# A new written-out order for the first half of a delta-rule and gated feed-forward kernel

## The chip, the cores and the metric

The kernel runs on one core of a Trainium2 chip. The metric is the device time of one execution in microseconds. Five engines run side by side: TensorE (PE in the profile, its weight loads PEld), VectorE (DVE), ScalarE (ACT), GpSimd (POOL) and SyncE (SP), which only issues transfers. Each engine works through its own instructions in the order in which the program gave them; semaphores make one engine wait for another.

## The reference, cut to what matters

```python
# q, k, v: (4, 8, 768, 48); beta: (4, 8, 768)
k_n = k / (norm(k) + 1e-06)
for t in range(768):                       # one state per batch and head
    y[t] = q[t] @ state
    v_old = k_n[t] @ state
    state = state + beta[t] * outer(k_n[t], v[t] - v_old)
x = y.transpose(0, 2, 1, 3).reshape(3072, 384)
h = x @ w_in                               # 384 x 2048
out = (h * cos(h)) @ w_out                 # 2048 x 384
```

All inputs are float32; the weights come as pairs of 32-bit words which the kernel joins to one.

## The kernel before, in words

The sequence is cut into 24 units of 32 steps (index n below); two units make a pair (index p or m, 12 of them), and one pair's outputs are the 256 tokens of one pass of the feed-forward part.

For a unit the kernel loads k, q and v (`("k", n)`, ...; `load`, L398), turns k and q (`turn`, or by blocks from memory: `("blocks", n, a)`, L417), forms the two Gram matrices (`gram`, L675; `gram_keys`, `gram_queries`) and needs the inverse of a triangular matrix made of the first. For units 0 and 1 that inverse is formed by repeated doubling on TensorE (`("double", n, level, par)`, L759, with copies on ScalarE, L767, and turns and adds on VectorE, L772 to L779). From unit 2 on it is formed for a pair at a time by column elimination on GpSimd: the Gram matrix goes to memory (`gram_put`, L833) and back in another layout (`gram_get`, L846 and L854), `eye` (L865, L867) sets the start, `("inv", m, i)` (L879, L886) are the steps, and the result goes to memory (`put`, L891) and back (`get`, L902 for pair 1 and L910 for the others). Of pair 1, the step `("inv", 1, 0)` runs on VectorE and the other three on GpSimd. The recurrence of a unit is then `state` (L930), `right`, `solve` (L996, L1002; for pair 1 it is `solve_half` and `between`, both L960, with `half_out` on ScalarE, L972, and `between_out` on VectorE, L980, after them), `solve_out` (L1014), `update` (L1027), `update_out`, `within` (L1045, L1057), `within_out` (L1070), `features` (L1078) and `features_out` (L1086). `norms` (L574), `scale` and `weigh` prepare the factors.

The feed-forward part of pair 0 is plain: `("hidden", 0, f)` (L1099) and `("out", 0, i, k)`. For the other pairs the first product is done as 20 block products, `("layer", p, x)` (L1273), of sums of the inputs, `("x_sum", p, name)` (L1188), the second as seven, `("out", p, step, part)` (L1355), with sums of gates `("left", p, x, s)` (L1371). `turns` (L1136), `rest` (L1143), `cos` (L1152) and `gate` (L1155) form h cos(h).

The weights arrive in 28 loads `("weights", t)` (L518): 12 of 512 KB for `w_in`, 16 of 384 KB for `w_out`. Each takes one of eight tiles of tag g, is split on ScalarE (`split`, L528 and L532), shifted on VectorE (`shift`, L536) and joined on GpSimd (`("add", t)`, L540), which frees the tile. The same eight tiles serve squares, gates and `half_out`.

`("warm", i)` (L495) is one matmul on data that nobody reads, a filler for TensorE; once an output product has begun it issues nothing:

```python
    def keep_warm():
        if not out_begun:
            nc.tensor.matmul(p_out[:, 0], ...)
```

There are five of them ahead of everything and 17 among the tasks.

All of this is written as 2199 tasks. `Order.add` registers a task under its key with its dependencies and the tiles it makes and uses; the costs, due times and engines that are handed to it are not used when the order is run. `Order.LINE` is the order itself: it names every task once, by its number in the order of registration, and `Order.run` calls them in that sequence. An engine therefore gets its instructions in the order of the line. `Order.run` also gives out the tiles: of a tag's free places the one that has been free longest. So the line also sets whose release a task waits for. `Order.OTHER` is a set of keys. A transfer whose key is in it is issued by ScalarE's queue, otherwise by SP's (`queue`); for `inv`, `x_sum`, `in_sums`, `left` and `right` it chooses between GpSimd and VectorE (`either`).

Of the kernel before, what the change touches and what calls it, by code (L numbers as in the profile page):

```python
# [59 lines left out]
class Order:  # L60

    OTHER = {
        ('v', 0), ('v', 1), ('gram_put', 2), ('gram_put', 3), ('inv', 1, 0), ('put', 1),
        ('gram_put', 4), ('v', 5), ('gram_get', 2), ('put', 2), ('gram_put', 6), ('v', 8),
        ('v', 9), ('blocks', 9, 0), ('blocks', 9, 1), ('put', 4), ('get', 10), ('v', 11),
        ('blocks', 11, 0), ('blocks', 11, 1), ('gram_put', 11), ('gram_get', 5), ('v', 12),
        ('gram_put', 13), ('gram_get', 6), ('get', 13), ('v', 14), ('blocks', 14, 0), ('v', 15),
        ('blocks', 15, 0), ('blocks', 15, 1), ('v', 16), ('gram_put', 16), ('v', 17), ('k', 18),
        ('v', 18), ('get', 18), ('v', 20), ('gram_put', 21), ('gram_get', 11), ('store', 0, 1),
        ('right', 4, 4), ('left', 1, 1, 0), ('left', 1, 3, 0), ('left', 1, 3, 1),  # L70
        ('store', 1, 0), ('store', 1, 1), ('x_sum', 2, 'd'), ('x_sum', 2, 'n'),
        ('x_sum', 2, 'm'), ('x_sum', 2, 'e'), ('x_sum', 2, 'k'), ('x_sum', 2, 'g'),
        ('x_sum', 2, 'i'), ('x_sum', 2, 'l'), ('x_sum', 2, 'f'), ('x_sum', 2, 'b0'),
        ('left', 2, 4, 1), ('left', 2, 3, 1), ('x_sum', 3, 'd'), ('x_sum', 3, 'n'),
        ('x_sum', 3, 'm'), ('x_sum', 3, 'e'), ('x_sum', 3, 'k'), ('x_sum', 3, 'g'),
        ('x_sum', 3, 'i'), ('x_sum', 3, 'l'), ('x_sum', 3, 'h'), ('x_sum', 3, 'b0'),
        ('left', 3, 4, 1), ('left', 3, 3, 1), ('store', 3, 0), ('store', 3, 1),
        ('x_sum', 4, 'd'), ('x_sum', 4, 'm'), ('x_sum', 4, 'g'), ('x_sum', 4, 'i'),
        ('left', 4, 3, 0), ('left', 4, 3, 1), ('x_sum', 5, 'd'), ('x_sum', 5, 'e'),
        ('x_sum', 5, 'l'), ('x_sum', 5, 'h'), ('x_sum', 5, 'b0'), ('left', 5, 2, 0),  # L80
        ('left', 5, 4, 1), ('left', 5, 3, 0), ('left', 5, 3, 1), ('x_sum', 6, 'd'),
        ('x_sum', 6, 'g'), ('x_sum', 6, 'l'), ('x_sum', 6, 'f'), ('x_sum', 6, 'b0'),
        ('left', 6, 1, 0), ('left', 6, 4, 0), ('store', 6, 0), ('x_sum', 7, 'd'),
        ('x_sum', 7, 'm'), ('x_sum', 7, 'g'), ('x_sum', 7, 'i'), ('x_sum', 7, 'f'),
        ('x_sum', 7, 'h'), ('x_sum', 7, 'b0'), ('left', 7, 4, 0), ('left', 7, 4, 1),
        ('left', 7, 3, 1), ('store', 7, 0), ('x_sum', 8, 'd'), ('x_sum', 8, 'm'),
        ('x_sum', 8, 'e'), ('x_sum', 8, 'k'), ('x_sum', 8, 'g'), ('x_sum', 8, 'l'),
        ('left', 8, 3, 0), ('store', 8, 0), ('store', 8, 1), ('x_sum', 9, 'd'),
        ('x_sum', 9, 'm'), ('x_sum', 9, 'e'), ('x_sum', 9, 'k'), ('x_sum', 9, 'i'),
        ('x_sum', 9, 'l'), ('x_sum', 9, 'b0'), ('left', 9, 1, 0), ('left', 9, 2, 0),  # L90
        ('left', 9, 1, 1), ('left', 9, 3, 0), ('store', 9, 1), ('x_sum', 10, 'k'),
# [1857 lines left out]
```

## Time and profile before

| | us |
|---|---|
| median of the runs (3) | 640.1 |
| lowest and highest | 638.85, 642.2 |
| profiled execution | 642.77 |
| its span, first to last instruction | 641.0 |

The profile is of one execution. Busy times and shares are of its span. In the list of groups a row gives line, engine, operation, the tile written and those read, the number of instructions, the busy time and the mean of one in ns, and the idle time just before them with what ended it. In the rows by stage the columns are from and to, the length, then for PE, PEld, DVE, ACT and POOL the busy time and the number of instructions, the mean granted clock of TensorE, the busy share of the DMA engines and GB/s. In the order of time a row begins with start and length. The chain of waits is followed back from the last instruction to whatever released each step.

### The profile page before, as it was taken

What the parts mean: (1) busy time and instruction counts of PE and PEld (TensorE: products, weight loads), DVE (VectorE), ACT (ScalarE), POOL (GpSimd) and SP (SyncE); (2) the same over time, 40 slices, a digit from 0 to 9 for tenths busy, and PEclk for the clock granted to TensorE, in tenths of its full rate; (3) what the DMA queues carried; (4) which work ended last, traced back from release to release, by engine and by line L of the source; (5) the groups of instructions that cost most, each with busy time, mean ns of one, the idle gap of its engine ahead of it and who ended that gap; (6) DMA issues with size and microseconds to landing.
All of it is one profiled execution on the core that took longest, in us unless ns stands there. A gap on an engine that the chain in (4) does not pass through costs nothing.

```text
span 641.0 us, 24058 instructions
## 1 busy us (share of the span) xinstructions
PE 612.1 (95%) x10096; PEld 571.4 (89%) x10096; DVE 504.4 (79%) x1051; ACT 297.5 (46%) x533; POOL 435.1 (68%) x791
## 2 busy tenths in 40 slices
PE   6978788999999999999999999999999999999997
PEld 4857777788799998999999999999999999999997
DVE  5876736999999897788878788978878676757872
ACT  3546535645543543543743553643544443635440
POOL 4428877788888888786886786888884881212231
PEclk8897979999999999999999999999999999999999
DMA  9876656655354645446234445333225011000001
GB/s 187 218 169 174 136 130 134 148 87 83 72 87 74 103 74 96 69 67 111 42 52 87 75 79 91 54 45 70 45 35 101 18 31 23 20 3 15 13 20 30
DMA packets 215844, 50.75 MB, mean 79 GB/s; under 512 B 207384, under 2 KB 210744, under 8 KB 215736
## 3 DMA queue, kind: packets, MB, share of 16 engines
q1 hardware_dynamic: 161132, 32.34, 27.8%
q10 hardware_dynamic: 54300, 16.33, 12.1%
q8 instruction: 79, 1.29, 0.8%
q0 software_dynamic: 304, 0.54, 0.4%
q14 instruction: 29, 0.24, 0.1%
HBM read 38.95 MB, written 10.22 MB: 77 GB/s over the span
## 4 chain that ended last, share of the span: by engine, by line
PE 76%; DMA 8%; POOL 5%; DVE 5%; issue 2%; SPq 2%; ACT 1%; ACTq 1%; DVEq 0%; POOLq 0%
PE p_out L1355 30%; PE p_h L1273 28%; PE p_kq L930 3%; PE p_s L1027 3%; POOL part L879 2%; POOL z L886 2%; PE p_u L1002 2%; PE p_kq L1057 2%; PE p_g L675 2%; PE p_h L1099 2%; DMA qp<-in_q_dram 2%; PE p_h L1355 2%; DMA kp<-in_k_dram 2%; PE p_z L1078 1%; DMA w_sum<-z_dr 1%
## 5 line engine op out<-in xcount | busy, mean ns | idle before, releaser
L879 POOL TENSOR_TENSOR part<-z,gb 128x126 f32<-128x126 f32 (+23 forms) x321 | 141.6, 441 | 44.1 <-DMA gb<-g_dr 17.5
L886 POOL TENSOR_TENSOR z<-z,part 128x126 f32<-128x126 f32 (+23 forms) x321 | 142.8, 445 | 25.2
L1355 PE MATMUL p_out<-w_out,g_ffn 128*128 128x192 f32 x672 | 121.0, 329 | 0.0
L1355 PEld LDWEIGHTS p_out<-w_out,g_ffn 128*128 128x128 f32 x672 | 107.9, 190 | 1.0
L1152 ACT ACTIVATE turns<-turns,halfpi 128x512 f32<-128x512 f32 x96 | 68.0, 718 | 83.2 <-DVE turns L1143 71.6
L1273 PE MATMUL p_h<-x_sum,w_in 128*128 128x128 f32 x704 | 92.3, 278 | 0.0
L1355 PE MATMUL p_out<-w_sum,g_ffn 128*128 128x192 f32 x496 | 88.7, 328 | 0.0
L1273 PEld LDWEIGHTS p_h<-x_sum,w_in 128*128 128x128 f32 x704 | 85.6, 191 | 1.9
L1136 ACT ACTIVATE turns<-g_ffn,quarter_turn 128x512 int32<-128x512 f32 x77 | 55.0, 719 | 66.3 <-DVE g_ffn L1155 35.4
L1355 PEld LDWEIGHTS p_out<-w_sum,g_ffn 128*128 128x128 f32 x496 | 79.6, 190 | 0.6
L1290 DVE TENSOR_TENSOR g_ffn<-g_ffn,p_h 128x512 f32<-128x512 f32 x88 | 59.5, 679 | 14.7 <-PE p_h L1273 13.7
L1155 DVE TENSOR_TENSOR g_ffn<-turns,g_ffn 128x512 f32<-128x512 f32 x77 | 61.7, 810 | 11.7 <-ACT turns L1152 11.6
L1143 DVE SCALAR_TENSOR_TENSOR turns<-g_ffn,turns 128x512 f32<-128x512 f32 x77 | 57.1, 750 | 8.2 <-ACT turns L1136 8.1
L1273 PE MATMUL p_h<-x_sum,in_sum 128*128 128x128 f32 x440 | 58.9, 278 | 0.8 <-POOL x_sum L1188 0.8
L1273 PEld LDWEIGHTS p_h<-x_sum,in_sum 128*128 128x128 f32 x440 | 54.3, 191 | 2.2 <-POOL x_sum L1188 1.0
L1070 ACT COPY y<-p_kq 32x384 f32<-32x384 f32 x96 | 45.1, 470 | 19.0 <-PE p_kq L1057 8.1
L1407 DVE SCALAR_TENSOR_TENSOR o<-p_out,o 128x192 f32<-128x192 f32 x74 | 25.1, 351 | 29.7 <-PE p_out L1355 29.5
L1273 PE MATMUL p_h<-x_ffn,w_in 128*128 128x128 f32 x352 | 46.6, 277 | 1.0 <-ACT p_h L1285 1.0
L1273 PEld LDWEIGHTS p_h<-x_ffn,w_in 128*128 128x128 f32 x352 | 43.0, 192 | 1.6 <-ACT p_h L1285 1.3
L574 POOL TENSOR_TENSOR knrm<-ksum,halves 128x16 f32<-128x16 f32 (+1 forms) x14 | 37.1, 2647 | 10.1 <-DVE ksum L562 9.5
L1371 POOL TENSOR_TENSOR g_ffn<-g_ffn 128x512 f32<-128x512 f32 x15 | 19.1, 1271 | 30.5 <-DVE g_ffn L1155 26.6
L1285 ACT COPY p_h<-p_h 128x512 f32<-128x512 f32 x44 | 25.3, 575 | 28.5 <-PE p_h L1273 20.4
(168 smaller groups left out, 1051.7 us busy)
## 6 DMA issues: line engine op xcount, KB each, us to landing
g_ffn<-in_moe_w_in_dram SPq DMA_DIRECT2D x7, 512.0 KB, 7.8
g_ffn<-in_moe_w_out_dram SPq DMA_DIRECT2D x9, 384.0 KB
kp<-in_k_dram SPq DMA_DIRECT2D x136, 24.0 KB, 2.5
gb<-g_dr SPq DMA_DIRECT2D x12, 256.0 KB, 3.9
g_ffn<-in_moe_w_out_dram ACTq DMA_DIRECT2D x7, 384.0 KB
g_ffn<-in_moe_w_in_dram ACTq DMA_DIRECT2D x5, 512.0 KB, 5.9
vp<-in_v_dram ACTq DMA_DIRECT2D x52, 48.0 KB, 2.7
zt<-z_dr SPq DMA_DIRECT2D x68, 32.0 KB, 2.7
```

Source lines behind the costliest of these rows:

```text
L574: nc.gpsimd.tensor_tensor(out=scales[m][2][:, part], in0=sums[m, part.start][:, 0:n], in1=halves[:, 0:n], op=ALU.pow,)
L879: eng.tensor_tensor(out=part, in0=z[:, 0:rows, j, None].to_broadcast(shape), in1=a[:, j, None, j + 1 :].to_broadcast(shape), op=ALU.mult,)
L886: eng.tensor_tensor(out=behind, in0=behind, in1=part, op=ALU.subtract)
L1070: nc.scalar.copy(by_parity(y[quarter(b)]), p_kq[quarter(b ^ 1), :, b % 2])
L1136: nc.scalar.activation(turns[p, f], hidden_of(p, f), AF.Identity, bias=quarter_turn, scale=TURN)
L1143: nc.vector.scalar_tensor_tensor(out=r, in0=hidden_of(p, f), scalar=TURN, in1=t, op0=ALU.mult, op1=ALU.subtract,)
L1152: nc.scalar.activation(r, r, AF.Sin, bias=halfpi, scale=2.0 * math.pi)
L1155: nc.vector.tensor_tensor(out=place(p, f), in0=step_of(rests.pop((p, f)), f), in1=step_of(hidden_of(p, f), f), op=ALU.mult,)
L1273: nc.tensor.matmul(p_h[:, e], in_block(*w)[:, e], x_of(p, b), start=new and e == 0, stop=True, skip_group_check=True,)
L1285: nc.scalar.copy(to, part_of(p, one))
L1290: nc.vector.tensor_tensor(out=part_of(p, to), in0=part_of(p, one), in1=part_of(p, two), op=op)
L1355: nc.tensor.matmul(p_o, left(p, part, a)[:, e % 4], right(e, b), start=(e == 0), stop=(e == FT // 2 - 1), skip_group_check=True,)
```

## The change

Only the two tables of `Order` are changed. The tasks, their instructions and their engines stay; no key of `x_sum`, `left`, `right`, `inv` or `in_sums` enters or leaves `OTHER`.

`OTHER`, as far as it changes: the keys that leave it (27, their transfers go from ScalarE's queue to SP's) and those that enter it (10).

```diff
-('gram_put', 2) ('gram_put', 3) ('gram_put', 6) ('gram_put', 13) ('gram_get', 5) ('gram_get', 6)
-('put', 4) ('get', 13) ('v', 1) ('v', 5) ('v', 8) ('v', 9) ('v', 11) ('v', 12) ('store', 1, 0)
-('blocks', 9, 0) ('blocks', 9, 1) ('blocks', 11, 0) ('blocks', 11, 1) ('blocks', 14, 0)
-('weights', 2) ('weights', 4) ('weights', 9) ('weights', 11) ('weights', 12) ('weights', 17) ('weights', 24)
+('gram_put', 5) ('get', 9) ('k', 5) ('k', 8) ('blocks', 12, 0)
+('weights', 1) ('weights', 7) ('weights', 8) ('weights', 10) ('weights', 21)
```

Counted in transfers, 43 more are issued by SP than before and 43 fewer by ScalarE.

`LINE`: the places up to the 1099th are written anew, nearly all of them with another task; from the 1100th on the line is the same to its end. Some lines of the diff, those around the inverse of pair 1 and unit 2:

```diff
-215 216 753 821 2140 2136 754 128 131 2133 2141 132 133 141 2130 217 284 2142 2148 134 135 233 2121
-2122 189 234 136 235 2126 2137 2138 262 2151 170 755 756 2149 2134 2144 236 2150 2152 238 20 153 825
-239 2155 266 237 2159 263 264 758 757 824 175 2163 759 240 137 2167 2171 2153 154 763 822 823 267
-138 2145 764 2146 2154 241 242 155 156 157 190 826 765 158 760 2156 768 159 160 761 2175 766 762 265
...
+2140 2122 2136 2147 753 2106 217 19 2148 188 2130 754 2125 131 2141 2142 132 2149 284 133 134 135
+821 189 2144 2151 233 234 235 2133 170 136 2145 154 25 236 237 758 755 238 2126 2137 756 153 262 757
+263 137 2150 239 175 2152 763 7 20 240 825 826 2155 2134 138 2159 823 155 156 2163 267 2146 768 759
+822 824 827 264 764 2160 2153 2167 157 765 766 158 2138 760 761 266 159 762 2171 190 287 160 2161
...
```

In these numbers 188 is `inv.1.3`, 189 `put.1`, 238 `gram_put.5`, 153 `get.2`, 156 `solve_half.2`, 158 `between.2`, 768 `hidden.0.6`, 159 `between_out.2`, 160 `solve.2`, 2122 `add.8`, 2106 `add.4`, 2147 `weights.15`, 2148 `split.15`, 753 `turns.0.0`, 170 `v.3`, 2151 `weights.16`. (A task is written here as its key with points, `inv.1.3` for `("inv", 1, 3)`.)

The moves that the steps of the prediction speak of, read from the two lines for each engine:

| engine | order before | order after |
|---|---|---|
| TensorE | turn.0 behind four fillers; gram.1 right behind double.0.0.1 | turn.0 behind one filler; gram.1 two fillers later |
| TensorE | double.0.3.1, double.0.4.1 at its 34th and 35th place | at its 24th and 26th |
| TensorE | solve_half.2, between.2, hidden.0.6, solve.2 | solve_half.2, hidden.0.6, between.2, solve.2 |
| TensorE | hidden.0.10, warm.13, state.3, features.2, warm.14, solve_half.3 | hidden.0.10, state.3, features.2, solve_half.3 |
| TensorE | solve.3, update.3 | solve.3, warm.13, update.3 |
| TensorE | out.0.0.0 behind all that emits a filler | warm.14 behind out.0.0.0 |
| TensorE | layer.2.3, layer.2.8, layer.2.9, solve.6, ..., out.1.0.1 | layer.2.9, layer.2.3, out.1.0.1, layer.2.8, solve.6 |
| GpSimd | add.4, ..., inv.1.1, inv.1.2, inv.1.3, ..., add.8 | inv.1.1, inv.1.2, add.8, add.4, inv.1.3 |
| GpSimd | left.1.1.0, x_sum.2.h | x_sum.2.h, left.1.1.0 |
| GpSimd | norms.7.0 behind inv.5.0 | norms.7.0 behind inv.6.0 |
| VectorE | scale.7.0 at its 328th place | at its 341st, gram_keys.14 still at its 343rd |
| ScalarE | eye.1, square.2.0, double_copy.1.4.1, within_out.0 | square.2.0, within_out.0, double_copy.1.4.1, eye.1 |
| ScalarE | weights.15, split.13, split.12, turns.0.0, gram_put.4, split.15, put.1 | weights.15, gram_put.4, split.15, turns.0.0, put.1 |
| SP | weights.16, v.3, gram_put.5, get.2 | weights.16, v.3, get.2 (gram_put.5 on ScalarE) |

Two of the tile places change owner with the line: the load `weights.15` had the tile that the square of pair 2 left (released by `sum.2.0`) and has the one that `weights.8` leaves (released by `add.8`); `x_sum`, bank and gate places move likewise without a change in number.

More of the change, by code (lines that the diff above doesn't have):

```diff
@@ L99 @@
-        ('weights', 15), ('weights', 17), ('weights', 23), ('weights', 24)
+        ('v', 0), ('inv', 1, 0), ('put', 1), ('gram_put', 4), ('k', 5), ('gram_put', 5),
+        ('gram_get', 2), ('put', 2), ('k', 8), ('get', 9), ('get', 10), ('gram_put', 11),
+        ('blocks', 12, 0), ('v', 14), ('v', 15), ('blocks', 15, 0), ('blocks', 15, 1),
+        ('v', 16), ('gram_put', 16), ('v', 17), ('k', 18), ('v', 18), ('get', 18), ('v', 20),
+        ('gram_put', 21), ('gram_get', 11), ('store', 0, 1), ('right', 4, 4), ('left', 1, 1, 0),
```

65 lines of the change are left out of this document (29 added, 36 removed), and 192 rows, old and new, of the table LINE.

## The prediction, made before the result was known

> **What bounds the kernel now.** I read the page first (busy shares, slices), then the busy time by stage, then what TensorE waited for in each stage, and last the chain of waits through the one long stall.
>
> From the page, the span, TensorE's share, and its 40 slices of 16 us with the granted clock beneath:
>
> ```profile
> span 641.0 us, 24058 instructions
> ...
> PE 612.1 (95%) x10096; PEld 571.4 (89%) x10096; DVE 504.4 (79%) x1051; ACT 297.5 (46%) x533; POOL 435.1 (68%) x791
> ...
> PE   6978788999999999999999999999999999999997
> ...
> PEclk8897979999999999999999999999999999999999
> ```
>
> TensorE is busy 612.1 of 641.0 us, so only 28.9 us can come out of any order, and the slices put nearly all of them in the first seven. The stages, one row each (from, to, length, then TensorE's busy time):
>
> ```profile
> 0.00:58.00 58.00, 44.59 (x909) 37.48 (x910) 43.18 (x133) 28.35 (x58) 27.58 (x37) 0.89 0.79 188
> 58.00:82.70 24.70, 18.67 (x369) 17.19 (x352) 17.41 (x34) 12.86 (x25) 19.50 (x28) 0.91 0.65 138
> 82.70:118.00 35.30, 31.60 (x939) 28.78 (x942) 20.46 (x46) 18.75 (x37) 29.24 (x67) 0.90 0.59 134
> 118.00:306.00 188.00, 185.94 (x3143) 167.79 (x3140) 168.83 (x344) 86.59 (x155) 157.36 (x294) 1.00 0.53 88
> 306.00:641.00 335.00, 331.34 (x4775) 320.13 (x4773) 254.50 (x497) 150.97 (x260) 201.38 (x368) 1.00 0.25 45
> ```
>
> Idle, by subtraction: 13.4, 6.0, 3.7, 2.1 and 3.7 us. The last moved task of the line stands at its 1099th place, which the kernel reaches at about 306 us; from there both orders are the same and TensorE is full, so the last row is a fixed 335 us. What the change can win lies in the first four rows, what it can lose has no such limit. In the second row the stall has one cause; this is the chain of waits over it:
>
> ```profile
> 71.03 0.43 DVE g L696
> ...
> 71.48 0.40 SPq L833
> ...
> 71.98 1.30 SPq L902
> ...
> 75.95 6.62 DMA w_sum<-z_dr
> ...
> 82.71 1.55 PE p_w L960 x59
> ```
>
> SP's queue held `get.2` (L902, eight transfers) behind `gram_put.5` (L833), which waited for a VectorE result of unit 5; the last transfer landed 82.57 and `solve_half.2` (L960) went on at 82.71. All of the work up to `hidden.0.4` is done by then in either order, so time won or lost before it counts only as far as it moves this landing: 82.7 us is a meeting point.
>
> **The change part by part.**
>
> *The meeting point.* Its two feeders are SP's queue and `put.1`. The rows of before, by engine:
>
> ```profile
> 68.17 1.90 SPq L398 DMA_DIRECT2D vp<-in_v_dram  x4
> ...
> 47.84 0.42 ACT L865 COPY z<-w_sum 128x256 f32<-128x256 f32 x1
> ...
> 52.61 0.95 ACT L1070 COPY y<-p_kq 32x384 f32<-32x384 f32 x2
> ...
> 64.30 0.38 ACTq L891 DMA_DIRECT2D z_dr<-z  x1
> 52.92 0.17 DVE L879 TENSOR_TENSOR part<-z,gb 128x15 f32<-128x15 f32 x1
> 63.40 0.23 POOL L886 TENSOR_TENSOR z<-z,part 128x15 f32<-128x15 f32 x1
> 63.58 1.29 POOL L540 TENSOR_TENSOR w_in<-w_in,g_ffn 128x512 uint32<-128x512 uint32 x1
> ```
>
> For it: `gram_put.5` goes to ScalarE's queue, so SP could begin `get.2` when `v.3` is issued, at 68.17 + 1.90 = 70.07, which is 1.9 us earlier. Against it, three things on the way to `put.1`. First, `eye.1` (L865) moves behind `within_out.0` and one double_copy: 52.61 + 0.95 + 0.38 + 0.42 = 54.4, and `inv.1.0`, 52.92 before, waits for it: +1.4 us. Second, `add.8` and `add.4` stand between `inv.1.2` and `inv.1.3` on GpSimd, 2 x 1.29 = +2.6. So the inverse of pair 1, done at 63.63, is done at 67.6. Third, ScalarE's queue now issues `weights.15` ahead of `split.15`, `turns.0.0` and `put.1`, and its tile is freed only by `add.8`: at about 61.72 + 1.4 + 1.29 = 64.4 (61.72 is the end of `inv.1.2`; its next step on `z` begins 61.80). `split.15` waits for that load. How long `put.1` and such a load take to land:
>
> ```profile
> DMA to landing us min/median/max: 2.9/4.0/6.6
> g_ffn<-in_moe_w_in_dram SPq DMA_DIRECT2D x7, 512.0 KB, 7.8
> ...
> g_ffn<-in_moe_w_in_dram ACTq DMA_DIRECT2D x5, 512.0 KB, 5.9
> ```
>
> With 4.0 us to land, `put.1` of before was there at 68.3, 3.7 us before `get.2` used it. Without the load, the new `put.1` issues at 67.6 and lands at 71.6: `get.2` 0.4 us earlier. With a load of 384 KB at the larger load's 5.9 us, 64.4 + 5.9 = 70.3, then 1.0 (split) and 0.7 (turns): `put.1` at 72.0, landing 76.0, 4.0 us later. Ends: -1.9 and +4.0 (with 7.8 us, +5.9). I take the middle of the two, **+1.0 us**, since the load is smaller than the one measured. Everything ahead of this (the doubling of units 0 and 1, where `double.0.3.1` comes forward by ten TensorE places and `gram.1` back behind two fillers) I cost at nothing: the meeting point hides it; without that cover its price would be its share of the first row's 13.4 us.
>
> *Behind it.* The rows of TensorE:
>
> ```profile
> 84.87 1.50 PE L960 MATMUL p_v<-g_ffn,in_sum 32*32 32x48 f32 x64 [0.62 <-ACT g_ffn L972]
> 86.30 4.62 PE L1099 MATMUL p_h<-x_ffn,w_in 128*128 128x128 f32 x24
> ...
> 96.17 2.94 PE L1099 MATMUL p_h<-x_ffn,w_in 128*128 128x128 f32 x24
> 98.95 0.60 PE L495 MATMUL p_out<-o 128*128 128x256 f32 x2
> 99.48 1.15 PE L930 MATMUL p_kq<-st,kq_t 48*64 48x48 f32 x64
> ...
> 103.86 0.88 PE L960 MATMUL p_v<-g_ffn,in_sum 32*32 32x48 f32 x64 [0.78 <-ACT g_ffn L972]
> ...
> 109.67 0.89 PE L1027 MATMUL p_s<-u,kp 64*64 64x96 f32 x32 [1.24 <-DVE u L1014]
> ```
>
> `hidden.0.6` changes places with `between.2`: it now covers the 0.62 us that waited for ScalarE, and no longer covers VectorE's answer ahead of `solve.2`. The nearest answers are 0.62 and 1.24, I take 0.8: **+0.2** (0.0 to +0.6). The filler `warm.13` (L495) leaves the full stretch at 98.95, 99.48 - 98.95 = **-0.5**, for the idle 1.24 ahead of `update.3`. `warm.14` moves behind the first output, where the code issues nothing; it stood in a wait (`features_out.2`), so that is 0.
>
> *118 to 306 us.* TensorE's waits there:
>
> ```profile
> PE p_h L1273 <- ACT p_h L1285: 1.0, 1, 1.0
> PE p_h L1273 <- POOL x_sum L1188: 0.8, 1, 0.8
> PE p_u L1002 <- DMA zt<-z_dr: 0.3, 1, 0.3
> ```
>
> The second is `layer.2.3` on `x_sum.2.h`; GpSimd now makes that sum ahead of `left.1.1.0`, and `layer.2.9` goes first: **-0.8**. The third is `solve.6`; `out.1.0.1` is put ahead of it: **-0.3**. Around the first the places stand: 0. New waits I bound by 0 and by one displaced step of GpSimd (the rival below), and take 0.
>
> *Queues.* 43 transfers' issues go from ScalarE's queue to SP's net; those shown here take about 0.48 us of the sequencer each (68.17: 1.90 for four). That frees ScalarE, which is 46% busy, and loads SP, which computes nothing. I take 0; the one place where it is on the path is `get.2` above.
>
> The sum: 1.0 + 0.2 - 0.5 - 0.8 - 0.3 = -0.4 us. The profiled execution took 642.8 us (641.0 and 1.8 around it), so 642.4; it stood 2.7 above the median of the runs shown, 640.1, and on that median the forecast is **639.7 us**.
>
> **The rivals.** Differences under 0.5% (3.2 us) are about what a measurement of this kernel can tell from no change.
>
> *B, the stall falls below what halves the clock: 634.5 us.* The two stretches:
>
> ```profile
> 78.60:82.70 4.10, 0.48 (x4) 0.29 (x5) 2.95 (x5) 0.69 (x1) 2.15 (x6) 1.00 0.62 127
> 83.00:89.80 6.80, 6.18 (x138) 5.87 (x135) 2.15 (x7) 2.58 (x5) 5.55 (x17) 0.50 0.89 254
> ```
>
> TensorE did 0.48 us of work in 4.1, and then had half the clock for 6.8 us. In it `hidden.0.6` took 4.62 for 2.94 and `between.2` 1.50 for 0.88: 2.3 us. If `get.2` comes the full 1.9 us earlier and the idle is short enough, the clock stays: -0.4 - (1.0 + 1.9) - 2.3 = -5.6, 634.5. For it: the order of SP's queue. Against: the longer way to `put.1`. The Trainium skill ("TensorE: Matmul & The Clock Gate", "Why this matters for your kernels") asks for no idle gap over about 3 us and says that one idle window brings half rate; by that rule, the trace agrees, an idle of 1.8 would keep the clock and one of 4.7 would not, which is this rival against the forecast.
>
> *C, `put.1` is stuck in ScalarE's queue: 644.6 us.* One mechanism: `weights.15` waits for `add.8`, `split.15` for `weights.15`, `put.1` stands behind both. With 7.8 us to land, `get.2` is 5.9 later: -0.4 - 1.0 + 5.9 = +4.5. It decides as soon as `put.1` issues after 71.98 - 4.0 = 68.0 us. For it: each engine's queue is in order. Against: the load is 384 KB, and the first 58 us may run ahead of the old ones.
>
> *D, a step moved too late: 643.1 us.* `norms.7.0` goes 16 places down GpSimd, behind `inv.6.0`; `gram.14`, at the same TensorE place, needs it through `scale.7.0`. One step costs:
>
> ```profile
> L574 POOL TENSOR_TENSOR knrm<-ksum,halves 128x16 f32<-128x16 f32 (+1 forms) x14 | 37.1, 2647 | 10.1 <-DVE ksum L562 9.5
> ```
>
> up to 3.4 us with its queue, if `gram.14` (275 us) has to wait for all of it: -0.4 + 3.4 = +3.0. That nothing at all changes, because one full engine does the same work, is inside the forecast.
>
> **How the numbers follow.** Forecast 0.40 (its own range 636.5 to 643), B 0.28, C 0.24, D 0.08. Faster by over 0.5% (under 636.9): B and a little of the forecast, 0.33. Slower (over 643.3): C, half of D, a little of the forecast, 0.34. Within: 0.33. The range leaves out the ends of B and C, with 0.1 on each side: 634 to 645.5.
>
> **What would show it.** `get.2` (L902) right behind `v.3` and landing between 80 and 87 us; `put.1` (L891) at 68 or later; one filler less (x38 on L495); no wait for `x_sum` or `zt` between 118 and 306; the granted clock halved after the stall (forecast, C) or not (B). From the 1100th task on, the same 335 us. I am wrong if the first 82 us move by more than the landing of `get.2`, or if TensorE has new waits behind 118 us.

## The result and the profile after

The changed kernel took **649.99 us** (median of 4 runs, 649.88 to 651.48), the kernel before 640.28 in the same session (4 runs, 638.85 to 642.2). The ratio is **1.0155, 95% interval 1.0124 to 1.0186**: 9.7 us slower. The forecast, 639.7 with a range of 634 to 645.5, missed it. The profiled execution took 651.48 with a span of 649.6 (before 642.77 and 641.0). In the profiles of the changed kernel and of all experiments but before_again a step's line number is three lower than before: `solve` is L999 for L1002.

The page of the changed kernel: span, busy shares, TensorE by slices of 16.2 us, and the granted clock.

```profile
span 649.6 us, 24058 instructions
...
PE 613.6 (94%) x10094; PEld 571.5 (88%) x10094; DVE 506.4 (78%) x1051; ACT 299.1 (46%) x533; POOL 438.5 (67%) x791
...
PE   7878797998899899999999999999999999999997
...
PEclk7998798999999899999999999999999999999999
```

The work is the same, but the full stretch no longer begins at slice 8: slices 10, 11 and 14 show gaps, and slice 14 a lower clock. The same stages as before (from and to, length, then busy time of PE, PEld, DVE, ACT, POOL, the clock, DMA share, GB/s):

```profile
0.00:58.00 58.00, 44.74 (x847) 36.28 (x849) 41.92 (x127) 29.27 (x59) 26.22 (x35) 0.91 0.80 189
58.00:82.70 24.70, 19.11 (x418) 17.78 (x411) 17.31 (x38) 11.42 (x24) 19.11 (x26) 0.86 0.67 143
82.70:118.00 35.30, 30.58 (x840) 27.07 (x839) 22.04 (x51) 19.74 (x39) 29.60 (x68) 0.95 0.59 132
118.00:306.00 188.00, 181.52 (x3166) 164.80 (x3165) 163.57 (x331) 86.02 (x152) 156.51 (x288) 0.99 0.47 80
306.00:649.60 343.60, 337.66 (x4843) 325.60 (x4841) 261.56 (x510) 152.64 (x262) 207.03 (x375) 1.00 0.26 48
```

Length less busy time gives TensorE's idle: 13.3, 5.6, 4.7, 6.5 and 5.9 us, where before had 13.4, 6.0, 3.7, 2.1 and 3.7. Up to 118 us that is 23.6 against 23.1, and by equal work (defined with the table of runs below) the changed kernel is 0.4 us ahead at 118 us: **the front, on which most of the prediction was spent, is close to a draw. The loss lies behind it**: +4.4 idle between 118 and 306, +2.2 behind 306, and one half-clock stretch at 221 us, 3.4 us long, where before has none behind the front. At half the clock such a stretch costs about half its length, 1.7 us (an estimate; its rows are in the last section). Together these are 8.3 us of the 8.6 by which the spans differ. Over the whole trace both kernels have the same time at half clock, 23.8 us: the front of the changed one has 3.4 us less of it.

TensorE's waits of the changed kernel from 118 to 306 us (total, times, longest):

```profile
PE p_u L999 <- DMA zt<-z_dr: 2.1, 2, 1.8
PE p_h L1270 <- ACT p_h L1282: 1.9, 2, 1.7
PE p_out L1352 <- DVE o L1404: 1.9, 1, 1.9
PE p_h L1270 <- ACT g_ffn L1284: 0.5, 1, 0.5
```

The wait for `x_sum` is gone as predicted. Others stand in its place; here are the three long ones in order of time, and behind them the longest of the last stage, from TensorE's timeline (start, length, the instruction, and in brackets the idle before it and its releaser):

```profile
152.94 0.28 PE L999 MATMUL p_u<-rhs,zt 64*64 64x48 f32 x2 [1.81 <-DMA zt<-z_dr]
...
178.74 1.49 PE L1270 MATMUL p_h<-x_sum,in_sum 128*128 128x128 f32 x11 [1.68 <-ACT p_h L1282]
...
220.94 2.68 PE L1352 MATMUL p_out<-w_out,g_ffn 128*128 128x192 f32 x8 [1.86 <-DVE o L1404]
...
321.84 1.13 PE L1270 MATMUL p_h<-x_sum,w_in 128*128 128x128 f32 x8 [1.21 <-ACT g_ffn L1284]
```

They are `solve.5`, `layer.2.9`, `out.1.6.0` and `layer.5.1`. Three of them are followed back one engine:

- `solve.5` waits for `get.5`, which SP issued at 149.59 behind a run of 24 transfers: `k.10`, `blocks.9.0`, `k.11` and `blocks.9.1`. The two `blocks` steps among them, eight transfers, are ones that the change took from ScalarE's queue. Before, `get.5` went out at 135.51. The last rows of SP after:

```profile
142.06 5.23 SPq L395 DMA_DIRECT2D kp<-in_k_dram  x8
147.33 2.15 SPq L414 DMA_DIRECT2D qp<-in_q_dram  x4
149.59 1.91 SPq L907 DMA_DIRECT2D zt<-z_dr  x4
```

and the row of SP before:

```profile
135.51 2.76 SPq L910 DMA_DIRECT2D zt<-z_dr  x4
```

- `layer.2.9` waits for ScalarE's `layer_out.2.7`, which stands in ScalarE's queue behind `eye.4` (L864), and `layer.5.1` for `layer_out.5.1` (321.10), which stands behind the transfers of `v.14` (313.80) and of an output (`store.3.0`, 319.67), both issued by ScalarE, and behind the `turns` steps that follow each. ScalarE's rows after:

```profile
149.02 0.84 ACT L554 ACTIVATE g_ffn<-kp 128x768 f32<-128x768 f32 x1 [6.73 <-DMA kp<-in_k_dram]
...
176.97 0.62 ACT L864 COPY z<-consts 128x512 f32<-128x512 f32 x1 [3.72 <-DMA z_dr<-z]
...
313.80 2.09 ACTq L395 DMA_DIRECT2D vp<-in_v_dram  x4
315.93 0.72 ACT L1133 ACTIVATE turns<-g_ffn,quarter_turn 128x512 int32<-128x512 f32 x1 [2.66 <-DMA vp<-in_v_dram]
...
320.36 0.72 ACT L1133 ACTIVATE turns<-g_ffn,quarter_turn 128x512 int32<-128x512 f32 x1 [1.76 <-DMA kp<-in_k_dram]
```

`eye.4` needs the `z` tile that `put.3` still reads. ScalarE is only 46% busy, yet it stood still for 6.73, 3.72, 2.66 and 1.76 us with steps behind it in its queue on which TensorE's next steps hang: the share of busy time told nothing of this. After the 6.73, for instance, come `square.5.0`, VectorE's `sum.5.0` and `gram_queries.8`, and the last frees the bank that `solve.5` writes.

Now the front, to set beside the prediction's rows: the timelines of TensorE, ScalarE, VectorE and SP of the changed kernel, a fence each:

```profile
69.64 0.66 PE L639 MATMUL p_t<-consts,kp 128*128 128x128 f32 x4 [2.44 <-DVE st L1032]
...
83.02 0.88 PE L957 MATMUL p_w<-rhs,w_sum 32*32 32x48 f32 x64
83.83 2.94 PE L1096 MATMUL p_h<-x_ffn,w_in 128*128 128x128 f32 x24
```

```profile
62.84 0.36 ACTq L515 DMA_DIRECT2D g_ffn<-in_moe_w_out_dram  x1
...
67.31 0.55 ACT L525 ACTIVATE w_out<-g_ffn 128x384 f32<-128x384 f32 x1 [7.33 <-DMA g_ffn<-in_moe_w_out_dram]
67.39 0.39 ACTq L888 DMA_DIRECT2D z_dr<-z  x1
```

```profile
67.89 0.84 DVE L533 TENSOR_SCALAR w_out<-w_out 128x384 uint32<-128x384 uint32 x1 [3.04 <-ACT w_out L525]
68.65 0.94 DVE L1032 TENSOR_TENSOR st<-st,p_s 128x768 f32<-128x768 f32 x1
```

```profile
68.76 1.91 SPq L395 DMA_DIRECT2D vp<-in_v_dram  x4
70.77 5.42 SPq L899 DMA_DIRECT2D w_sum<-z_dr  x8
```

`weights.15` (issued 62.84) holds `split.15` (67.31) and with it `put.1` (67.39), as the prediction's rival C has it; SP issues `get.2` right behind `v.3`. The row of `solve_half.2` at 83.02 has no idle ahead of it, where before it had to wait until 82.71. The 3.7 us of idle are gone from there, but `turn.5` has 2.44: its feeder `update_out.1` (L1032) stands in VectorE's queue behind `shift.15` (L533), which waited 3.04 for `split.15`. The clock has changed its places too, in the rows by stage of the changed kernel:

```profile
70.97:77.80 6.83, 5.14 (x137) 4.81 (x138) 4.98 (x9) 4.83 (x10) 3.40 (x4) 0.50 0.51 78
```

Behind that stretch the clock is full until 101.7 us: `hidden.0.6`, the row at 83.83, takes 2.94 us and `between.2` 0.88, where before they ran at half and took 4.62 and 1.50. The half clock lies ahead of `solve_half.2` instead of behind it.

### The profile page after: what moved, and what is told of

Same layout as the page of the kernel before. It is cut to its first block, busy times and chain, and to the rows that moved or that the text cites. A ratio compares the mean times of both kernels' runs of the same rounds, so it can differ in the third digit from the quotient of the medians.

```text
span 649.6 us, 24058 instructions
## 1 busy us (share of the span) xinstructions
PE 613.6 (94%) x10094; PEld 571.5 (88%) x10094; DVE 506.4 (78%) x1051; ACT 299.1 (46%) x533; POOL 438.5 (67%) x791
## 4 chain that ended last, share of the span: by engine, by line
PE 76%; DVE 4%; DMA 3%; SPq 2%; issue 1%; ACT 1%; POOL 1%; ACTq 0%; POOLq 0%
PE p_h L1270 29%; PE p_out L1352 29%; PE p_kq L927 3%; PE p_s L1024 2%; PE p_kq L1054 2%; PE p_h L1096 2%; PE p_g L672 2%; PE p_u L999 2%; PE p_out L1294 2%; PE p_h L1352 2%; PE p_z L1075 1%; DMA gb<-g_dr 1%; DVE turns L1140 1%; SPq L414 1%; DMA z_dr<-z 1%
## 5 line engine op out<-in xcount | busy, mean ns | idle before, releaser
L883 POOL TENSOR_TENSOR z<-z,part 128x126 f32<-128x126 f32 (+23 forms) x321 | 145.3, 453 | 25.2
L1352 PE MATMUL p_out<-w_out,g_ffn 128*128 128x192 f32 x672 | 123.0, 331 | 2.1 <-DVE o L1404 2.1
L1133 ACT ACTIVATE turns<-g_ffn,quarter_turn 128x512 int32<-128x512 f32 x77 | 55.3, 721 | 71.6 <-DVE g_ffn L1152 33.4
L1152 DVE TENSOR_TENSOR g_ffn<-turns,g_ffn 128x512 f32<-128x512 f32 x77 | 63.0, 823 | 9.1 <-ACT turns L1149 9.0
L1140 DVE SCALAR_TENSOR_TENSOR turns<-g_ffn,turns 128x512 f32<-128x512 f32 x77 | 58.5, 767 | 11.6 <-ACT turns L1133 11.4
L1067 ACT COPY y<-p_kq 32x384 f32<-32x384 f32 x96 | 45.2, 470 | 20.5 <-PE p_kq L1054 13.4
```

What stands on the lines that cost most here:

```text
L883: eng.tensor_tensor(out=behind, in0=behind, in1=part, op=ALU.subtract)
L1067: nc.scalar.copy(by_parity(y[quarter(b)]), p_kq[quarter(b ^ 1), :, b % 2])
L1133: nc.scalar.activation(turns[p, f], hidden_of(p, f), AF.Identity, bias=quarter_turn, scale=TURN)
L1140: nc.vector.scalar_tensor_tensor(out=r, in0=hidden_of(p, f), scalar=TURN, in1=t, op0=ALU.mult, op1=ALU.subtract,)
L1152: nc.vector.tensor_tensor(out=place(p, f), in0=step_of(rests.pop((p, f)), f), in1=step_of(hidden_of(p, f), f), op=ALU.mult,)
L1352: nc.tensor.matmul(p_o, left(p, part, a)[:, e % 4], right(e, b), start=(e == 0), stop=(e == FT // 2 - 1), skip_group_check=True,)
```

## The experiments

The theories as they stood at first: **S**, the loss is the sum of the four late steps above; **Q**, it is the queue table; **O**, it is the order; later **V**, that VectorE's order leaves no slack (the expectations call it theory D, and their C is a kernel that is short of slack everywhere; these aren't the prediction's rivals C and D). In the table, "busy" is TensorE's busy time in the fixed window 118 to 306 us of the profiled run (before 185.94, after 181.52), "lost" is how much later than in the first trace of before TensorE has done the same work at 335 us, less the same at 130 us. (For this each TensorE step is given its shortest duration over all the traces, and the sums along the two orders are compared.) The ratios are to runs of before on the same chip.

| run | us | ratio (95%) | busy | lost |
|---|---|---|---|---|
| order_new_queues_old | 667.81 | 1.0451 (1.0414, 1.0488) | 173.29 | 22.2 |
| order_old_queues_new | 644.18 | 1.0050 (1.0017, 1.0082) | 186.32 | -0.2 |
| front_new_rest_old | 644.09 | 1.0070 (1.0043, 1.0097) | 182.85 | 2.3 |
| front_old_rest_new | 648.28 | 1.0127 (1.0097, 1.0158) | 182.37 | 8.1 |
| get5_ahead | 651.51 | 1.0183 (1.0145, 1.0221) | 180.84 | 8.4 |
| eye4_collect | 651.14 | 1.0169 (1.0128, 1.0210) | 182.18 | 7.1 |
| v14_blocks17 | 649.23 | 1.0149 (1.0106, 1.0192) | 180.07 | 8.9 |
| four_moved_back | 649.13 | 1.0147 (1.0104, 1.0191) | 182.41 | 8.5 |
| get5_bank_two | 649.01 | 1.0150 (1.0113, 1.0186) | 182.58 | 7.0 |
| ten_moved | 652.11 | 1.0195 (1.0152, 1.0238) | 181.01 | 6.5 |
| before_gram_put5 | 639.48 | 0.9997 (0.9972, 1.0021) | 185.69 | -0.5 |
| before_again | 637.95 | one run | 186.69 | -0.6 |
| light_old | 638.60 | 0.9989 (0.9963, 1.0014) | 187.86 | -2.3 |
| light_new | 644.17 | 1.0100 (1.0070, 1.0129) | 184.69 | 4.2 |
| pool_new | 647.24 | 1.0151 (1.0111, 1.0191) | 183.12 | 5.3 |
| pool_old | 655.49 | 1.0268 (1.0242, 1.0295) | 175.25 | 16.5 |
| six_moved | 651.95 | 1.0176 (1.0141, 1.0210) | 180.89 | 8.8 |
| light_six_moved | 646.94 | 1.0107 (1.0075, 1.0140) | 183.71 | 5.0 |

### Which table: the line or the queues

```diff
 order_new_queues_old
-OTHER of after
+OTHER of before
 order_old_queues_new
-LINE of after
+LINE of before
```

> The new line of order with the old choice of queue (the 43 issues go back to ScalarE). Theory Q (the loss comes from SP's queue, which got 43 issues more of about 0.5 us each, so that short transfers such as get.5, gram_put.9 and k.19 come late): 640 to 643 us, no wait of solve.5 for get.5, and the 8.5 us that TensorE lost behind 130 us are gone. Theory O (the line itself puts single steps too late on their engines, whichever queue issues): 648 to 651 us, with get.5 still the wait of solve.5. In between, 643 to 648, if the two are about equal.

> The old line of order with the new choice of queue (43 issues go from ScalarE to SP, nothing else). Theory Q: 646 to 650 us, SP late by 10 us or more behind 118 us. Theory O: 638 to 642 us, as before. The prediction took 0 for this part.

Measured 667.81 and 644.18. The new line with the old queues is the slowest of all. TensorE's and ScalarE's timelines of order_new_queues_old show the place, which alone is 6.7 us:

```profile
143.36 1.01 PE L1270 MATMUL p_h<-x_sum,w_in 128*128 128x128 f32 x3 [6.74 <-ACT g_ffn L1282]
```

```profile
139.78 2.02 ACTq L414 DMA_DIRECT2D qp<-in_k_dram  x4
141.85 0.55 ACT L525 ACTIVATE w_out<-g_ffn 128x384 f32<-128x384 f32 x1 [8.04 <-DMA kp<-in_k_dram]
...
142.74 0.57 ACT L1282 COPY g_ffn<-p_h 128x512 f32<-128x512 f32 x1
```

ScalarE has to issue `blocks.9.0`, which goes out only at 139.78 and stands among loads of keys: the releaser that the trace names for ScalarE's 8.04 us of idle is such a load. `layer_out.1.12`, for which TensorE waits, stands behind it, and 10.2 us at half clock follow. So neither Q nor O holds. The queue table alone costs 3.2 us by the ratio (1.1 to 5.2), where the prediction took 0; its one trace loses nothing between 130 and 335 us, so where these 3.2 arise is open. And the new line needs the new table, since without it the loss more than doubles (27.7 us for 9.7). The two tables are one object.

### Which places: the front or the rest

```diff
 front_new_rest_old
 places 1 to 460 of after's line
-places 461 on, in after's order
+places 461 on, the remaining tasks in before's order and queues
 front_old_rest_new
-places 1 to 460 of after's line
+places 1 to 460 of before's line
 places 461 on, the remaining tasks in after's order and queues
```

> The new order and the new queues for the first 460 places (to about 131 us), behind them the old order and queues. The traces put TensorE's loss in that front at -0.6 to +0.1 us, so 639 to 642 us by both theories; 644 or more would say that the front leaves something behind (tiles, SP's backlog) that only shows later.

> The old order and queues for the first 460 places, behind them the new ones. By the traces the whole loss is here: 648 to 651 us by both theories; below 645 would say that the loss needs the new front as well.

Measured 644.09 and 648.28. The loss of front_new_rest_old behind 130 us, 2.3 us, lies at the seam, in its timeline of TensorE:

```profile
133.13 0.89 PE L1024 MATMUL p_s<-u,kp 64*64 64x96 f32 x32 [2.23 <-DVE u L1011]
```

From 146 us on it keeps step with before. front_old_rest_new loses 8.1 us behind 130 us, as the whole change does (8.4), and has the same stalls at `layer.2.9`, `out.1.6.0`, `layer.5.1` and `layer.5.9`. So most of the loss belongs to the rest of the line. The front isn't cleared by this: 644.09 is what its expectation named as the sign that the new front leaves something behind, and the two parts cost 0.7% and 1.3% where the whole costs 1.55%. front_old_rest_new hasn't the stall of `solve.5`: that one needs the new front.

### Theory S: the late steps put back

```diff
 get5_ahead, SP
+get.5
 blocks.9.0  k.11  blocks.9.1
-get.5
 eye4_collect, ScalarE and VectorE
-eye.4   three layer_out of pair 2
+three layer_out of pair 2   eye.4
-layer_out.2.36  rest.2.(1,0,0)  x_sum.3.n  x_sum.3.i  collect.1.3
+collect.1.3  layer_out.2.36  rest.2.(1,0,0)  x_sum.3.n  x_sum.3.i
 v14_blocks17, ScalarE and SP
+v.14 behind features_out.11, blocks.17.0 ahead of put.6
-v.14 and blocks.17.0 at after's places
 four_moved_back
+all five of these moves
```

> The changed kernel with one step moved: on SP get.5 right behind blocks.8.0, ahead of k.10, blocks.9.0, k.11 and blocks.9.1. Both theories of the first four runs fell (queues old on the new line: 667.8). New theory S: the loss is a handful of single steps that stand too late on their own engine; solve.5 waited 2.1 us for get.5, so 647.5 us (650.0 - 2.4), and no idle ahead of solve.5. Rival C: the new order is short of slack everywhere, the time comes back at the next step: 649.3 us or more.

> The changed kernel with two steps moved: eye.4 on ScalarE behind layer_out.2.9 (it stood, waiting for put.3 to be read out of the one z tile, ahead of layer_out.2.3 and 2.7), and collect.1.3 on VectorE ahead of layer_out.2.36. S: the idle ahead of layer.2.9 (1.68) and out.1.6.0 (1.86) goes, and the half clock behind the second (3.4 us of it, 1.5 us of work): 650.0 - 5.0 = 645.0 us. C: 648 us or more.

> The changed kernel with the two transfers moved that stand latest ahead of the 1100th task: v.14 on ScalarE right behind features_out.11 (before: just ahead of turns.4.(1,1,0)), blocks.17.0 on SP ahead of put.6. S: layer.5.1 (1.21) and layer.5.9 (0.47) no longer wait, the part behind the 1100th task is again 335 us or close to it: 648.0 us (650.0 - 2.0). C: 649.3 us or more.

> All the moves of the three kernels before this one together: five steps of 2199. S: the sums add, 650.0 - 2.4 - 5.0 - 2.0 = 640.6 us, 639 to 643. C: 645 us or more, with new waits of TensorE in other places of 130 to 330 us.

Measured 651.51, 651.14, 649.23 and 649.13: **S falls**. Each move did what it was to do at its place: `layer.2.9` and `out.1.6.0` have no wait in eye4_collect, and v14_blocks17 loses 0.4 us instead of 2.4 between 306 and 335. Yet none of them is faster. For get5_ahead and v14_blocks17 the gains expected, 2.4 and 2.0 us, are no larger than what the intervals leave open (2.4 to 2.8 us to either side); for all five moves, 9.4 us expected, the answer is clear. In get5_ahead `solve.5` is still late, in TensorE's timeline:

```profile
152.28 1.48 PE L999 MATMUL p_u<-rhs,zt 64*64 64x48 f32 x32 [1.67 <-issue]
```

and SP's rows of the same trace tell why:

```profile
144.63 3.81 SPq L395 DMA_DIRECT2D kp<-in_k_dram  x8
148.48 2.35 SPq L414 DMA_DIRECT2D qp<-in_q_dram  x4
```

`get.5` is out of the way, but the load `k.11` now begins 144.63 and not 142.06, ScalarE's `square.5.0` waits for it, and behind that stands the release of the bank that `solve.5` writes. ("issue" means that the trace names no releaser; the bank is read from the order of the tasks.) In eye4_collect new waits come up at `solve.10` (1.31) and `layer.4.4` (1.24), in four_moved_back at `layer.2.1`, `layer.3.1`, `out.2.5.0` and `layer.4.4` (0.8 to 0.9 each), and there `solve.5` keeps 1.71, with 6.8 us at half clock behind it.

### The bank as well, and ten steps

```diff
 get5_bank_two = get5_ahead and, VectorE
+gram_queries.8 right behind right.5
-gram_queries.8 behind sum.5.0
 ten_moved = four_moved_back, get5_bank_two and, VectorE and ScalarE
+layer_out.3.1 ahead of turns.2.(1,0,0);  collect.2.5 ahead of gate.3.(1,0,0)
+layer_out.4.5 ahead of turns.3.(1,0,1);  update_out.1 ahead of shift.15
```

> The changed kernel with two steps moved that meet at solve.5: get.5 on SP behind blocks.8.0 as in the run before, and gram_queries.8 on VectorE right behind right.5 instead of behind sum.5.0. Solve.5 writes the one bank that gram_queries.8 has to free, and that waited through sum.5.0 and square.5.0 for the load k.11. Theory S2 (the places have two or three late steps each, and all have to be moved): no idle ahead of solve.5, 650.0 - 2.4 = 647.6 us, 2 us less again where the idle had cost the full clock. C: 649.5 us or more.

> The changed kernel with ten steps moved: the five of the last run of the second set and gram_queries.8, layer_out.3.1, collect.2.5, layer_out.4.5 and update_out.1, each to just ahead of the step behind which it made TensorE wait in the trace of that run. S2: 649.1 - 1.7 - 2.8 (full clock behind solve.5) - 0.8 - 0.8 - 0.9 - 1.0 = 641 us. C (short of slack everywhere): 645 us or more, again with new places.

Measured 649.01 and 652.11. In get5_bank_two `solve.5` has no wait any more; instead `layer.1.2`, right beside it, waits 1.90 us for a VectorE step behind `sum.5.0`. Ten steps put where the trace wants them, each at a place where TensorE was seen waiting, gain nothing. ten_moved loses little up to 222 us, then 4.6 us between 260 and 306, at `solve.10` (1.42, for `get.10`) and `layer.4.1` (1.69), where after had lost nothing. In these runs a wait taken away in one place was followed by one at another step.

### The front's own terms, and the spread

```diff
 before_gram_put5
-OTHER of before
+OTHER of before and ('gram_put', 5)
 before_again
 (before, unchanged)
```

> The kernel before with gram_put.5 alone moved from SP to ScalarE, behind square.3.0. The prediction took 1.9 us for it (SP free for get.2), and 5.8 with the clock kept. If SP's queue decides: get.2 issued from about 70.1 us and landing by 81, 634 to 638 us. If the landing of the eight transfers decides, not their issue: 639.5 to 640.5 us, as before.

> The kernel before once more, for a second trace: its 20 runs beside the first four kernels lie between 636.3 and 645.0 us, and the one profiled was 2.7 above their middle. If the landing of get.2 carries the spread, the idle ahead of solve_half.2 (3.7 us in the first trace) differs by what the time differs, within 1 us, and the stages behind 118 us are the same within 0.5 us.

before_gram_put5 took 639.48: 0.9997 of before (0.9972 to 1.0021). SP did get free early:

```profile
66.23 1.93 SPq L395 DMA_DIRECT2D vp<-in_v_dram  x4
68.26 4.73 SPq L899 DMA_DIRECT2D w_sum<-z_dr  x8
```

`get.2` began 3.7 us ahead of before's 71.98, and the time of the whole kernel is the same (-1.8 to +1.3 us by the interval), so the prediction's -1.9 (and B's -5.6, which hangs on it) isn't seen in it. Its one trace is 4.2 to 4.8 us ahead of before's first by equal work at 84 us, but the second trace of before is 3.1 to 3.8 ahead there without the move; and it gives 2.9 us back between 440 and 540 us, where the order is the old one. What the move is worth in the front alone can't be told from the spread. A second profile of before is of a run of 637.95, 4.8 us less than that of the first, and its windows say where:

```profile
0.00:58.00 58.00, 45.37 (x946) 37.97 (x947) 44.29 (x136) 29.63 (x60) 28.51 (x38) 0.94 0.79 190
...
118.00:306.00 188.00, 186.69 (x3215) 169.60 (x3214) 169.79 (x346) 88.22 (x157) 159.80 (x302) 1.00 0.50 86
```

In the first 58 us the clock is 0.94 against 0.89. By equal work it is 2.6 us ahead at 62 us, 3.8 at 84, and 4.3 to 4.8 from 118 to the end. The two traces of before differ by their half clock: 13.7 us in the whole trace here, 23.8 in the first. The 10.2 us less, at half speed, are an estimated 5.1, about all of the 4.8. With it the landing moved too: SP issued `get.2` at 70.92, for 71.98, and `solve_half.2` went on at 78.80, for 82.71. So this pair doesn't speak against the prediction's "meeting point".

### Theory V: less work for VectorE, and one engine's order alone

In light_old and light_new VectorE's step `rest` is left out for pairs 1 to 4.

```diff
 light_old (with before's tables), light_new (with after's)
 r = rests[p, f] = t.bitcast(FP)
+if 1 <= p <= 4: return
 pool_new (before's tables, but GpSimd's steps behind place 460 in after's order)
 pool_old (front_old_rest_new, but GpSimd's steps behind place 460 in before's order)
```

> The order before, with the step rest (one VectorE instruction of 0.7 us, between two of ScalarE) left out for all blocks of pairs 1 to 4: 32 instructions, 23 us of VectorE, and the hand-over to it and back. That part of the gate is then not computed. TensorE is full there, so all theories: 636 to 640 us, as before or a little less.

> The changed kernel with the same step left out for pairs 1 to 4. Theory D (VectorE and ScalarE hand their results to TensorE with no time to spare in the new order): relief gives the slack back, within 3 us of the old order with the same step out, so 638 to 643 us. Rival (TensorE's own order, the queues or GpSimd carry the loss): still 7 us or more above it, 646 to 650 us.

> The kernel before, with GpSimd's order alone taken from the change behind the 460th place; all other engines and queues as before. If GpSimd's order carries the loss: 645 to 648 us. Theory D: 639 to 641 us.

> The old order up to the 460th place, behind it the new one for all engines and queues but GpSimd, which keeps its old order. It goes with the run that was old in front and new behind (648.3). If GpSimd's order carries the loss: 640 to 642 us. Theory D: 647 to 649 us.

Measured 638.6, 644.17, 647.24 and 655.49. The old order gains nothing from a lighter VectorE (0.9989, 0.9963 to 1.0014), the new one does: its ratio falls from 1.0155 to 1.0100 (1.0070 to 1.0129), which is 3.5 us, and its lost time from 8.4 to 4.2. But light_old's own lost time fell by 2.3 as well, so of the 4.2 that the new order gets back only 1.9 are its own. So a quarter to a half of the loss depends on `rest`: V holds in part. Leaving `rest` out takes away VectorE's load and also a hand-over from ScalarE to VectorE and back; the two aren't told apart. The loss between 180 and 222 is gone (3.9 to -0.4), the stalls at `solve.5`, `layer.2.9`, `layer.5.1` and `layer.5.9` aren't.

GpSimd's order has no good version by itself either. Up to 335 us pool_new's loss is at one place, in TensorE's and VectorE's timelines:

```profile
266.61 1.42 PE L1024 MATMUL p_s<-u,kp 64*64 64x96 f32 x32 [3.55 <-DVE u L1011]
```

```profile
263.06 0.29 DVE L600 TENSOR_TENSOR knrm<-knrm,tiny 128x16 f32<-128x16 f32 x1 [4.80 <-POOL knrm L571]
```

This is the prediction's rival D, in another kernel: VectorE stands 4.80 us at `scale.7.0` for GpSimd's `norms.7.0`, `solve_out.10` stands behind it, and TensorE loses 3.55, close to the 3.4 that D forecast at most. In the change it didn't happen, because `scale.7.0` is later there too: `norms.7.0` was done at 272.64 and `scale.7.0` began at 276.52. pool_old loses 15 us between 180 and 222, with waits of 4.80 at `layer.3.15` and 6.34 at `out.1.6.0` and 13.7 us at half clock in the whole trace. Its 655.49 rules out GpSimd's new order as the carrier of the change's loss: with the old one it is slower still.

### Both at once

```diff
 six_moved = four_moved_back and gram_queries.8 right behind right.5
 light_six_moved = six_moved, and rest left out as in light_new
```

> The changed kernel with six moves: get.5, eye.4, collect.1.3, v.14 and blocks.17.0 as in the run four_moved_back, and gram_queries.8 behind right.5; nothing left out. Two causes (late single steps, and no time to spare on VectorE and ScalarE): 646 to 650 us, since the second is untouched. Late steps alone: 640 to 643 us.

> The same six moves with the step rest left out for pairs 1 to 4, as in light_old and light_new. Two causes: within 2 us of light_old (638.6), so 638 to 641 us. A third cause in TensorE's own order or in GpSimd's: 642.5 us or more.

Measured 651.95 and 646.94, and the theory that the loss is those six steps plus VectorE's load (638 to 641) falls too. TensorE's, VectorE's and ScalarE's timelines of light_six_moved:

```profile
153.23 1.51 PE L1270 MATMUL p_h<-x_ffn,in_sum 128*128 128x128 f32 x8 [2.06 <-DVE g_ffn L1152]
```

```profile
151.63 0.95 DVE L559 TENSOR_REDUCE ksum<-g_ffn 128x16 f32<-128x768 f32 x1 [4.23 <-ACT g_ffn L554]
```

```profile
150.75 0.84 ACT L554 ACTIVATE g_ffn<-kp 128x768 f32<-128x768 f32 x1 [9.49 <-DMA qp<-in_q_dram]
```

Now `layer.1.2` waits for VectorE's `gate.1.(0,0,0)`, VectorE stands 4.23 us for ScalarE's `square.5.0`, and that 9.49 us for loads on SP. `square.5.0` needs the load `k.11`, which SP issues from 142.78 to 147.70; the releaser that the trace names is the load right behind it, of `blocks.9.1`. It is the same place and the same load with another victim. In light_six_moved SP issues from 136.01 to 154.63 with pauses of at most 0.34 us: it is `get.5` that holds TensorE when it is late, and `k.11`, through `square.5.0`, when `get.5` is ahead. After and its repairs lose some 1.5 to 5 us between 146 and 160 us by equal work (ten_moved about 1); before and front_old_rest_new lose none there.

## Why the prediction was wrong

**The step that failed** is the one of the part "118 to 306 us": "New waits I bound by 0 and by one displaced step of GpSimd (the rival below), and take 0." The stage has 4.4 us more idle, and 1.7 of half clock after one of the waits: 6.1 us. The bound was wrong in kind. It looked for one late step on GpSimd, as rival D does, while behind the front the places 461 to 1099 of the line were written anew, and the waits came from SP's queue (`solve.5`, 1.81), ScalarE (`layer.2.9`, 1.68) and VectorE (`out.1.6.0`, 1.86), none of them from `norms.7.0`. The prediction had itself named this sign of being wrong, that TensorE has new waits behind 118 us. The numbers for a better bound stood in the profile of before: the row 118 to 306 has 2.1 us of idle in 188, so there was almost nothing to gain there, and everything to lose.

- **The meeting point, +1.0: near in size by luck, wrong in mechanism.** The row of `solve_half.2` lies at 83.02, 0.3 later than the end of its wait before, but it waits for nothing there: `get.2` was issued 1.2 us earlier (70.77 for 71.98), and in none of the eleven traces with the new front and queues does `solve_half.2` wait for it. So in the new order this is no meeting point, and the steps ahead of it, which the prediction put at nothing because the wait would hide them, count: `turn.5` has 2.44. `put.1` was issued at 67.39, just under C's deciding 68.0; C's chain (`weights.15`, issued 62.84 for an estimated 64.4, `split.15`, `put.1`) is there in the rows, but what it cost went to `turn.5` through VectorE. The low end, -1.9, doesn't follow from the prediction's own numbers: it let `put.1` land at 71.6, which leaves 0.4 before the old 71.98. Tried alone, `gram_put.5` doesn't change the time.
- **"Only 28.9 us can come out of any order": incomplete.** It counts TensorE's idle and leaves out the half clock, 23.8 us of before's trace and so an estimated 11.9 us lost, although rival B counts 2.3 of it.
- **"Time won or lost before counts only as far as it moves this landing": not refuted.** before_again was ahead at 62 us and still was at 118, but its landing had moved too. What the prediction didn't reckon with is the spread of this kernel: runs of before went from 634.9 to 643.2 on one chip, and between its two traces the half clock accounts for the difference.
- **`hidden.0.6`/`between.2` +0.2, `warm.13` -0.5: not refuted.** L492 has 38 instructions as forecast. At equal work the changed kernel is 0.4 us ahead at 118 us, when its trace is set beside before's first; no run takes these two terms alone.
- **`x_sum.2.h` -0.8 and `solve.6` -0.3: both waits went,** and didn't make the kernel faster.
- **Queues, 0: wrong.** The table alone costs 3.2 us (1.1 to 5.2) with the old line, at places that no run shows. With the new line it is what keeps 667.81 from happening, so its cost in the change itself can't be told as one number. What was left out is the place in the queue: SP "computes nothing", but in these traces it issued in order, and `get.5` stood behind the transfers of four steps. How full the queue is doesn't tell it: from 140 to 160 us SP spends 17.4 us on issues in the changed kernel, 15.5 before, and 17.9 in order_old_queues_new, which loses nothing there. The Trainium skill ("DMA: Bandwidth & Descriptors", "Issuing engines are not separate DMA queues") says that issuing from several engines saves only the sequencer's issue time, usually small beside the transfer; here one issue is small too, 1.91 us for the four of `get.5`, but issues add up in a queue, to 5.23 us for the eight transfers of `k.11` ahead of it.
- **The tail, "the same 335 us": wrong by 2.2 us.** The order is the same from the 1100th task, the state isn't: `v.14` was issued at place 1035 before and 1097 now, and its four issues hold ScalarE until 315.88. With that load and `blocks.17.0` moved back, in v14_blocks17, the 306 to 335 loss is 0.4 instead of 2.4.
- **The rivals.** B came in half: its sign is there, full clock behind `solve_half.2`, 2.3 us shorter on `hidden.0.6` and `between.2`, but 6.8 us at half clock lie at 71.0 to 77.8 instead; the front has 20.4 us at half clock (6.8, 3.4, 6.8, 3.4) for 23.8 before (10.2, 6.8, 6.8). C happened as a chain and not as a price. D didn't happen in the change; in pool_new it did. None of the four had the mechanism that decided, so the range was too narrow for a reason, not by chance.

**What is shown:** nearly all of the loss lies behind 130 us; most of it belongs to the new rest of the line with its table; no set of single late steps that was tried holds it; leaving out `rest` on VectorE gives back a quarter to a half; at 150 us the place in SP's queue is the cause, that of `get.5` or, with `get.5` ahead, that of `k.11`. **What stays open:** the remaining half or more, what the new front adds, and where the table's 3.2 us arise. A count fits, though it is no proof: of some 190 TensorE steps between 130 and 335 us, those whose last feeder on another engine ended less than 0.5 us ahead of them are 20 to 25 in the kernels with the old rest of the line (pool_new 27), and 34 to 44 in those with the new one (light_new 31). It separates the two groups and doesn't follow the size of the loss: ten_moved has 44 and loses 6.5 us, order_new_queues_old 34 and loses 22.2. It would fit that the new order has less slack on many steps at once, so that each repair uncovers the next; this isn't shown. No kernel with the new front or the new rest was faster than before; before_gram_put5 equals before.

## What to carry to other kernels

In a stretch where the bounding engine is already 99% busy, reordering all its feeders had almost nothing to gain here and cost 1 to 4.5 per cent: count how many of its steps have less than half a microsecond of slack before and after, queue by queue, as a warning, and don't price "new waits" at 0. ScalarE stood still with its whole queue while a transfer at the head of it wasn't issued yet (8.04 us in order_new_queues_old), so a half-idle engine or one that "computes nothing" can be the cause; read the place of each issue in its queue, not the busy share. A cut in the order is not a cut in the state: loads that are late at the cut, such as `v.14` here, are still late behind it.

## What was not expected of the hardware

**The half clock comes on a grid.** In every one of the 20 traces the stretches at half clock begin and end on a grid of 3.41 us that lies differently in each run; in the changed kernel they start at 9.5, 53.9, 71.0, 101.7 and 221.2 us. Whether a cell is at half goes with TensorE's work in the cell before it. Windows of the changed kernel, laid on its grid to within 0.1 us (second number after the length: TensorE's busy time; third last: clock):

```profile
98.37:101.78 3.41, 2.03 (x115) 1.68 (x117) 1.24 (x4) 1.55 (x3) 3.41 (x5) 0.99 0.47 72
101.78:105.20 3.42, 3.42 (x46) 3.30 (x35) 1.16 (x2) 1.00 (x2) 3.03 (x7) 0.51 0.74 164
149.57:152.98 3.41, 1.60 (x6) 0.64 (x5) 3.08 (x5) 1.52 (x3) 2.86 (x8) 1.00 0.55 79
152.98:156.40 3.42, 3.11 (x48) 2.94 (x48) 1.90 (x4) 1.34 (x3) 3.03 (x6) 1.00 0.26 48
217.84:221.25 3.41, 1.55 (x14) 1.39 (x13) 3.19 (x7) 1.94 (x4) 3.41 (x2) 0.99 0.50 82
221.25:224.66 3.41, 3.41 (x15) 3.41 (x14) 3.21 (x8) 3.14 (x6) 0.49 (x2) 0.51 0.84 197
```

After 1.55 busy the next cell is at half, after 1.60 it isn't; after 2.03 it is, but that was work in 32-row tiles. Over the 20 traces, leaving out the first 4 us, of the cells at full clock with less than 1.4 us of TensorE work all 37 were followed by half clock, of those with 1.4 to 2.1 us 41 of 90, of those with more none of some 3500. So a stall of 1.9 us would cost 1.9 or, with a cell at half behind it, an estimated 3.6 (1.9 and half of 3.4), by where the grid happens to fall. Between the two traces of before the half clock (13.7 us for 23.8) accounts for about all of the difference. Behind 118 us, 11 of the 13 traces with the new rest of the line and that of pool_new have a stretch at half clock, and none of the six with the old rest. The Trainium skill ("TensorE: Matmul & The Clock Gate", "What's actually happening") gives a free-running window of 3413 ns, and the traces agree with it; the rule of "HAM oscillation — how this bites in real kernels", no idle gap over about 3.4 us, is not enough here: 1.86 us of idle in one gap, and 0.76 and 0.62 in two, went ahead of half clock.
